# The h product of batches 6 and 7 in 512-token pieces, their loads in halves, and a new written order, in a fused linear-attention and gated-FFN kernel

## The chip, the cores and the metric

The kernel runs on one core of a Trainium2 chip. A core has five engines that run side by side, each through its own list of instructions in order: TensorE (PE, matrix products into PSUM), VectorE (DVE), ScalarE (ACT), GpSimd (POOL, which here issues the loads) and SyncE (SP, which here issues the stores). The metric is device time in microseconds for one execution. The kernel before took 179.14 us (median of 3 runs, 178.89 to 179.23).

## The reference

For 8 batches, 8 heads, 576 positions and 64 channels per head, the reference computes a linear attention, normalises it, joins the heads to 512 features, and sends the result through a feed-forward block whose gate is a convolution over three neighbouring positions:

```python
kv = np.einsum('bhsd,bhse->bhde', k, v)
out = np.einsum('bhsd,bhde->bhse', q, kv)
rms = np.sqrt(np.mean(out * out, axis=-1, keepdims=True) + 1e-06)
x = out / rms * g_norm              # heads joined: (8, 576, 512)
h = np.maximum(x @ w_in, 0.0)       # (8, 576, 1024)
conv_out = sum over k of conv_w[k] * (h moved by k - 1 positions)
gate = 1.0 / (1.0 + np.exp(-conv_out))
result = h * gate @ w_out           # (8, 576, 512), float32
```

## The kernel before, in words

**Order.** The whole program is written out by hand in one string, `ORDER` (lines 71 to 135). Each word names a function and its arguments; behind `@` stand the buffer slots that it takes, behind `!` the engine of a copy (`A` for ACT, `V` for DVE). The words are run in turn (lines 663 to 669) and each emits instructions. At the end (lines 671 to 679) the instructions of each engine are tied to that sequence, so every engine works strictly in the order of its own words. Between engines only data and buffer dependencies hold. The order comes from a search outside the kernel, which worked with a duration for every operation.

**Loads.** `Lq`, `Lk`, `Lv` (line 352) bring q, k, v of a batch from DRAM into SBUF, converted from float32 to bfloat16. With a second argument, `Lq.5.1`, one half of a batch (4 of 8 heads), otherwise the whole batch. Each of q, k and v has two slots, so a batch's load waits until the batch two or so before it in that slot has been read. `Li` and `Lo` bring the weights. All are issued by POOL, in order. The first half of batch 0 comes by another way: SP loads it as float32 into a staging tile and `ca` converts it.

**Attention.** `kv` multiplies k and v (36 small matmuls of 64x64 per half), `kvc` copies the result to SBUF, `qt` and `qc` transpose q (36 transposes per half, one copy), and `ot` (8 matmuls) gives the attention output of two head pairs in PSUM.

**Normalisation.** Batches 0 and 1 take a short way: `sq` squares (ACT), `on` sums (PE), `nl` is the reciprocal root (ACT), and `mz` scales into x (DVE). The later batches are normalised in pairs: `sq` and `oc` (ACT) square and copy the output, `ss` sums (PE), `ln` is the root (ACT), `sl` splits it into two bfloat16 parts (four DVE instructions), `sp` spreads it over the partitions (PE), and `mu` scales into x (DVE). The pairs are 2 and 3 (group 1), 4 and 5 (group 2), 6 and 7 (group 3). ACT loads one table for roots and another for the sigmoid and changes between them.

**h.** x of two batches lies in one tile of 1152 tokens. There are two ways to form h = relu(x w_in) for one block f of 128 features of the eight:

- `hm.b.f.u` (line 529): one batch, 576 tokens in two runs of 288; each `u` takes two of four contraction steps, 4 matmuls of 288 columns. It takes two PSUM banks. `re` applies the relu to 576 columns.
- `ha.p.f.e` (line 543): 512 of the pair's 1152 tokens, 4 matmuls of 512 columns, one PSUM bank; `rea` does the relu. The last 128 tokens of the pair come from `hb.p.j` (line 556), for four blocks f in one bank, 16 matmuls of 128 columns, and `reb`. The piece e=1 holds the last 64 tokens of the first batch and the first 448 of the second.

Before the change, batches 0, 1, 6 and 7 use `hm`, and the pairs p=1 (batches 2, 3) and p=2 (4, 5) use `ha` and `hb`.

**Gate.** For each group c of one or two batches (`CONV`, line 62) and each pair of feature blocks, DVE does `ta` (two scaled copies per block), `aa` and `ab` (two additions), ACT does `sg` (sigmoid), and DVE does `mg` (h times gate, in place). Groups 4 and 5 are batches 6 and 7.

**Output.** `om.p.k.i.j` (line 614) multiplies a tile of 128 tokens by half of w_out, 4 matmuls of 512 columns for i=0 (feature blocks 0 to 3) or i=1 (4 to 7). `ea` copies the finished tile into one of four row buffers in SBUF and `st` stores it, by SP. A row buffer is free again when its store has landed. The last token tile, `om.3.6`, is done in two halves of 256 columns. `sw.x.b` holds the next store back until the named load has landed. `STORES2` lists the outputs stored as two DMAs of 256 KB rather than one of 512 KB.

**Fillers.** `fi`, `fq` and `fo` are matmuls on zeros, put where PE would have nothing to do in the first part of the kernel.

Of the kernel before, what the change touches and what calls it, by code (L numbers as in the profile page):

```python
# [68 lines left out]


ORDER = """
pre@0,0,0 Lq.0.1 ca.q.0!V ca.q.1!V fi.36.128@0 fi.3.128@0 qt.0.0@0 qc.0.0!V@0 fi.1.512@2 fi.20.128@2 ct@0 ca.k.1!V
ca.k.0!A pn Lv.0.1 ca.v.0!V Lq.1.1@1 ca.v.1!A fq.1.512.0@1 fq.1.256.0@1 kv.0.0@1 Li.2 kvc.0.0!A pc fq.2.512.3@3
ot.0.0@6,4 ca.k.2!A sq.0.0@0 Li.0 fi.3.512@1 fi.2.128@1 on.0.0@0 nl.0.0@0 ca.k.3!V fq.2.512.0@2 fq.1.256.0@2 qt.0.1@2
qc.0.1!V@0 sq.0.1@0 mz.0.0@0 fi.1.512@0 fi.3.128@0 on.0.1@0 nl.0.1 fo.1.384.0.1 kv.0.1@2 kvc.0.1!V Lq.1.0 Li.3
fo.1.384.0.1 fq.1.256.1@6 ot.0.1@6,0 sq.0.2@0 mz.0.1 fq.1.512.0@2 qt.1.1@2 Li.1 Lv.1.0@1 fi.2.128@4 on.0.2@4 sq.0.3@7
nl.0.2@0 qc.1.1!V@0 fo.2.384.0.2 on.0.3@2 nl.0.3 Lk.1.0@1 fo.1.384.0.3 hm.0.5.0@4 mz.0.2 Lq.2.0@0 hm.0.4.0@2 mz.0.3
hm.0.1.0@6 hm.0.5.1 re.0.5!A@0 hm.0.4.1 ta.0.5@0 hm.0.1.1 re.0.4!A ta.0.4 qt.1.0@0 hm.0.0.0@2 hm.0.0.1 hm.0.3.0@4
hm.0.3.1 re.0.1!A ta.0.1@1 Lv.1.1 hm.0.6.0@6 qc.1.0!A@1 Lv.2.1@0 re.0.0!A aa.0.2 hm.0.2.0@0 hm.0.2.1 ab.0.2
fq.1.512.0@2 kv.1.0@2 sg.0.4 ta.0.0 re.0.3!V aa.0.0 Lk.1.1 sg.0.5 ab.0.0 kvc.1.0!A hm.0.6.1 re.0.2!A ot.1.0@4,2  # L80
hm.0.7.0@0 mg.0.2 re.0.6!V sg.0.0 Lq.3.1@1 sq.1.1@0 Lq.2.1 hm.0.7.1 ta.0.3@0 re.0.7!V ta.0.2 qt.2.0@6 qc.2.0!V@1
sq.1.0@1 aa.0.1 fo.5.384.1.1 on.1.0@0 sg.0.1 mg.0.0 nl.1.0@0 fo.5.384.1.0 on.1.1@6 nl.1.1 fo.2.384.1.0 kv.1.1@0
kvc.1.1!A fo.1.384.1.1 fq.1.256.2@6 ot.1.1@0,6 mz.1.0 mz.1.1 sq.1.2@0 qt.3.1@4 sq.1.3@1 Lk.2.1@0 qc.3.1!V@0 Lv.2.0
ab.0.1 on.1.2@2 nl.1.2@0 fo.2.384.1.2 on.1.3@4 nl.1.3 Lk.2.0 mz.1.2 fo.1.384.1.3 hm.1.7.0@2 qt.2.1@4 mz.1.3 hm.1.5.0@0
ta.0.6@1 sg.0.2 ta.0.7 hm.1.7.1 hm.1.5.1 sg.0.3 qc.2.1!V@2 re.1.7!A hm.1.1.0@6 hm.1.1.1 hm.1.4.0@4 Lv.3.1@1 re.1.1!A
hm.1.4.1 aa.0.3 mg.0.1 re.1.5!A kv.2.0@6 re.1.4!A Lo.0 hm.1.2.0@0 hm.1.2.1 ab.0.3 sg.0.6 sg.0.7 hm.1.6.0@2 ta.1.5@0
ta.1.4 Lk.3.1@1 kvc.2.0!V hm.1.6.1 Lo.1 ot.2.0@4,6 re.1.2!A re.1.6!A Lq.3.0 oc.2.1@0 kv.2.1@0 kvc.2.1!A Lq.5.0@0
hm.1.3.0@2 aa.1.2 mg.0.3 hm.1.3.1 sq.2.1@0 hm.1.0.0@0 hm.1.0.1 ta.1.7@1 sq.2.0@1 oc.2.0 ab.1.2 sg.1.5 om.0.0.0.0@7
sg.1.4 re.1.3!V ta.1.6 re.1.0!V ot.2.1@5,3 oc.2.3@1 sq.2.3@2 Lq.5.1 kv.3.1@0 om.0.0.0.1@2 aa.1.3 mg.1.2 om.0.0.1.1
Lk.3.0 sq.2.2@3 oc.2.2 kvc.3.1!V ot.3.1@0,3 ta.1.0@0 Lv.3.0 ea.0.0.1!A@0 ab.1.3 ta.1.1 qt.3.0@5 sg.1.7 sg.1.6  # L90
qc.3.0!V@0 oc.3.3@2 aa.1.0 mg.1.3 sq.3.3@4 om.0.1.1.0@2 oc.3.2 ta.1.3@1 om.0.1.0.0 ea.0.1.0!A@1 Lk.5.1@0 Lq.4.1@1
ta.1.2 om.0.1.0.1@6 om.0.0.1.0 ab.1.0 sq.3.2@5 ea.0.0.0!A aa.1.1 ab.1.1 om.0.1.1.1 sg.1.0 qt.5.1@0 qt.5.0@2 kv.3.0@4
qc.5.1!V@1 sg.1.1 ea.0.1.1!V qc.5.0!V@2 kvc.3.0!A Lq.4.0 om.0.2.1.1@7 mg.1.0 sg.1.3 sg.1.2 ot.3.0@0,4 om.0.2.1.0@6
sq.3.1@6 om.0.3.1.1@2 Lv.5.1@0 sq.3.0@7 ss.2@3 ss.3 ln.1@0 mg.1.1 oc.3.1@3 oc.3.0 sl.1@0 om.0.2.0.1 om.0.3.0.1 st.0.0
ea.0.3.1!A@2 kv.5.1@4 qt.4.1@0 Lk.5.0 sp.3.1.1@2 kvc.5.1!V Lk.4.1@1 mu.3.1.1@0 sp.2.0.1@4 mu.2.0.1 om.0.2.0.0
qc.4.1!A@0 sp.3.0.0@0 sp.3.1.0@2 ea.0.2.1!A@0 om.0.3.1.0@7 sp.3.0.1@4 mu.3.0.0 Lv.5.0 sp.2.1.1@0 mu.3.1.0 om.0.3.0.0
mu.3.0.1 sp.2.1.0@2 ea.0.2.0!A sp.2.0.0@4 mu.2.1.1 mu.2.0.0 mu.2.1.0 hb.1.0@6 Lv.4.1@1 fq.1.256.0@0 kv.4.1@0
ea.0.3.0!A kv.5.0@4 reb.1.0!A@1 kvc.5.0!V ot.5.1@6,2 kvc.4.1!A sq.5.2@0 oc.5.2@0 sq.5.3@1 ha.1.3.0@0 rea.1.3.0!V
ha.1.3.1@1 rea.1.3.1!V oc.5.3 ta.2.3@0 Lk.4.0 ot.5.0@6,4 ha.1.2.0@0 Lv.4.0 rea.1.2.0!V ha.1.2.1@3 oc.5.0@1 rea.1.2.1!V
ta.2.2 sq.5.1@2 Lk.7@0 oc.5.1 aa.2.1 ha.1.1.1@1 kv.4.0@4 sq.5.0@3 rea.1.1.1!A ot.4.1@6,2 kvc.4.0!A qt.4.0@0 oc.4.2@2  # L100
sq.4.3@4 qc.4.0!V@0 ab.2.1 oc.4.3 sq.4.2@5 ha.1.1.0@4 rea.1.1.0!A ta.2.1@1 ha.1.0.0@5 rea.1.0.0!A ha.1.0.1@2
ot.4.0@0,3 rea.1.0.1!A ta.2.0 aa.2.0 sq.4.1@6 sq.4.0@7 ha.1.6.0@5 ha.1.5.1@2 ss.4@6 oc.4.1@3 oc.4.0 ss.5 rea.1.5.1!A
ln.2@0 Lq.7@0 qt.7.1@3 qc.7.1!A@0 qt.7.0@0 om.0.4.0@2 sl.2@0 om.0.4.1 ab.2.0 ha.1.5.0@3 Lv.7@0 rea.1.6.0!A sp.5.0.1@4
sp.5.1.1@6 mu.5.0.1@1 qc.7.0!A@1 Lv.6@1 ea.0.4!A@3 sp.4.1.1@0 mu.4.1.1 ha.1.4.0@2 rea.1.5.0!A sg.2.0 hb.1.1@3 Lq.6@1
# [34 lines left out]
def kernel(  # L139
# [501 lines left out]
    def st(p, k, c=None):  # L641
# [68 lines left out]
```

## Time and profile before

| what | value |
|---|---|
| time, median of 3 runs | 179.14 us |
| the profiled execution, its own time | 179.12 us |
| its span, first to last instruction | 177.3 us |
| PE busy | 170.3 us (96%) |
| DVE busy | 157.0 us (89%) |
| ACT busy | 139.7 us (79%) |
| POOL busy (issuing loads) | 34.7 us (20%) |
| granted TensorE clock | 0.999 |

The profile gives busy times per engine, the same in 40 slices of the span, groups of instructions by source line and shape, the waits between engines, and a timeline. The duration of an instruction is longer than the distance to the next one on the same engine where the two overlap, so for an engine that works without a pause the distance from one start to the next is what an instruction costs. The 1.8 us between the span and the time lie outside the instructions.

### The profile page before, as it was taken

Reading aid. Unit: us, or ns where it says so; the run is one execution under the profiler, and the core shown is the slowest. Engines: PE = TensorE matmul, PEld = TensorE weight load, DVE = VectorE, ACT = ScalarE, POOL = GpSimd, SP = SyncE. Lnnn points to the kernel's source line nnn. Section 1 sums busy time; section 2 is a strip of 40 time slices with the busy share of each in tenths; the row PEclk is TensorE's granted clock in tenths of the full one; section 3 lists DMA queues with packets and bytes.
Section 4 is the critical chain, followed back from the end, with each engine's and each line's share of the span. In section 5 each row is a group of like instructions: output and inputs, shape, how many; then the busy total and the mean of one; then the engine's idle time right before and its main releaser. Section 6 shows DMA issues by size and latency. Waiting matters only on the chain.

```text
span 177.3 us, 5289 instructions
## 1 busy us (share of the span) xinstructions
PE 170.3 (96%) x2253; PEld 95.4 (54%) x2253; DVE 157.0 (89%) x282; ACT 139.7 (79%) x219; POOL 34.7 (20%) x60
## 2 busy tenths in 40 slices
PE   7999998899999999999999999999999999999992
PEld 7755765576444454444554454444577754444451
DVE  2757699999999796999999999999999999999931
ACT  2366799899999938999999999987795966494720
POOL 6945640851067005500000000000000000000000
PEclk9999999999999999999999999999999999999999
DMA  5999999999999996999881000005710000043594
GB/s 184 366 201 200 202 206 210 202 206 208 206 207 233 230 206 88 207 210 205 183 301 64 0 2 4 0 3 213 272 49 0 0 0 4 0 172 123 218 379 173
DMA packets 21355, 27.22 MB, mean 153 GB/s; under 512 B 1224, under 2 KB 15828, under 8 KB 21332
## 3 DMA queue, kind: packets, MB, share of 16 engines
q0 software_dynamic: 15072, 15.09, 51.5%
q1 hardware_dynamic: 6256, 11.80, 18.0%
q8 instruction: 17, 0.28, 0.6%
q14 instruction: 6, 0.05, 0.1%
q10 hardware_dynamic: 4, 0.00, 0.0%
HBM read 32.52 MB, written 9.44 MB: 237 GB/s over the span
## 4 chain that ended last, share of the span: by engine, by line
PE 66%; DVE 14%; DMA 8%; ACT 7%; issue 2%; POOL 1%; ACTq 0%; DVEq 0%
PE banks L628 28%; PE banks L534 13%; PE banks L547 12%; DMA v_sb<-in_v_dram 6%; PE banks L296 3%; PE banks L441 2%; ACT sq L448 2%; PE banks L393 2%; ACT h L238 2%; DVE xT L518 2%; DMA out_dram<-row 2%; PE banks L418 2%; DVE taps L583 2%; DVE taps L596 2%; DVE taps L584 1%
## 5 line engine op out<-in xcount | busy, mean ns | idle before, releaser
L628 PE MATMUL banks<-w_out_sb,h 128*128 128x512 bf16 x280 | 63.7, 379 | 0.2
L603 ACT ACTIVATE taps<-taps,cw 128x576 bf16<-128x576 bf16 (+1 forms) x48 | 43.6, 946 | 9.9 <-DVE taps L596 9.8
L628 PEld LDWEIGHTS <-h 128*128 128x128 bf16 x280 | 26.5, 98 | 31.5 <-issue 1.6
L238 ACT ACTIVATE h<-banks 128x512 bf16<-128x512 f32 (+1 forms) x51 | 29.8, 658 | 5.7 <-PE banks L534 4.2
L534 PE MATMUL banks<-xT,w_in_sb 128*128 128x288 bf16 x256 | 33.5, 286 | 0.4
L547 PE MATMUL banks<-xT,w_in_sb 128*128 128x512 bf16 x128 | 30.1, 379 | 0.2 <-ACT row L232 0.2
L534 PEld LDWEIGHTS <-w_in_sb 128*128 128x128 bf16 x256 | 24.6, 98 | 8.3 <-issue 1.6
L232 ACT ACTIVATE row<-banks 128x512 f32<-128x512 f32 (+1 forms) x29 | 16.8, 601 | 9.6 <-PE banks L628 5.6
L590 DVE TENSOR_TENSOR taps<-taps 128x1152 bf16<-128x1152 bf16 (+1 forms) x24 | 22.9, 956 | 0.5
L596 DVE TENSOR_TENSOR taps<-taps,h 128x1152 bf16<-128x1152 bf16 (+1 forms) x24 | 22.8, 952 | 0.3
L609 DVE TENSOR_TENSOR h<-h,taps 128x1152 bf16<-128x1152 bf16 (+1 forms) x24 | 22.7, 951 | 0.2 <-ACT taps L603 0.2
L583 DVE TENSOR_SCALAR taps<-h,cw 128x576 bf16<-128x576 bf16 (+1 forms) x48 | 20.3, 423 | 1.7 <-ACT h L238 1.5
L448 ACT ACTIVATE sq<-banks 128x576 bf16<-128x576 f32 x32 | 20.4, 674 | 1.7 <-PE banks L441 1.7
L584 DVE TENSOR_SCALAR taps<-h,cw 128x576 bf16<-128x576 bf16 (+1 forms) x48 | 20.1, 418 | 0.0
L547 PEld LDWEIGHTS <-w_in_sb 128*128 128x128 bf16 x128 | 11.8, 98 | 14.4 <-issue 1.3
L518 DVE SCALAR_TENSOR_TENSOR xT<-o,cw,banks 128x576 bf16<-128x576 f32 x24 | 18.1, 806 | 0.4 <-PE banks L511 0.3
L232 ACT ACTIVATE o<-banks 128x576 f32<-128x576 f32 x24 | 15.9, 678 | 0.0
L240 DVE TENSOR_SCALAR h<-banks 128x576 bf16<-128x576 f32 (+1 forms) x17 | 12.2, 720 | 1.1 <-PE banks L547 1.0
L354 POOL DMA_DIRECT2D k_sb<-in_k_dram x12 | 8.7, 726 | 20.0 <-PE banks L441 9.4
L227 ACT ACT_TABLE_LOAD x8 | 10.3, 1283 | 2.1 <-issue 2.0
L354 POOL DMA_DIRECT2D v_sb<-in_v_dram x13 | 9.4, 724 | 11.2 <-PE banks L324 4.7
L354 POOL DMA_DIRECT2D q_sb<-in_q_dram x13 | 9.6, 738 | 7.5 <-PE banks L418 6.5
(74 smaller groups left out, 149.1 us busy)
## 6 DMA issues: line engine op xcount, KB each, us to landing
out_dram<-row SPq DMA_DIRECT2D x10, 512.0 KB, 2.8
out_dram<-row SPq DMA_DIRECT2D x15, 256.0 KB, 4.1
q_sb<-in_q_dram POOLq DMA_DIRECT2D x11, 288.0 KB, 10.6
v_sb<-in_v_dram POOLq DMA_DIRECT2D x11, 288.0 KB, 10.7
k_sb<-in_k_dram POOLq DMA_DIRECT2D x10, 288.0 KB, 10.8
stg<-in_k_dram SPq DMA_DIRECT2D x2, 576.0 KB, 6.0
k_sb<-in_k_dram POOLq DMA_DIRECT2D x2, 576.0 KB, 10.1
q_sb<-in_q_dram POOLq DMA_DIRECT2D x2, 576.0 KB, 9.9
```

The lines of the kernel that those rows point to most:

```text
L232: nc.scalar.activation(to, fr, AX.Copy)
L238: nc.scalar.activation(to, fr, AX.Relu)
L354: loads[x, b] = nc.gpsimd.dma_start(out=qkv(x, b)[:, w0:w0 + n, :], in_=rows(x, b, w0, n))
L448: nc.scalar.activation(by_r(s), natural(T["ot", b, t][:, :S]), AX.Square)
L534: nc.tensor.matmul(ps[:, e, :HS], w_in_sb[:, t, f * P:(f + 1) * P], x[:, t, e * HS:(e + 1) * HS], start=(t == 0), stop=(t == NT - 1))
L547: nc.tensor.matmul(ps, w_in_sb[:, t, f * P:(f + 1) * P], x[:, t, e * 512:(e + 1) * 512], start=(t == 0), stop=(t == NT - 1))
L583: nc.vector.tensor_scalar_mul(tap[:, 0, f % 2, :n, 8:8 + S], h[:, f], cw[:, f:f + 1])
L590: nc.vector.tensor_add(tap[:, 1, :, :n, :S], tap[:, 0, :, :n, 7:7 + S], tap[:, 1, :, :n, 1:1 + S])
L596: nc.vector.tensor_add(y, y, h[:, 2 * j:2 * j + 2])
L603: nc.scalar.activation(y, y, AX.Sigmoid, scale=scale)
L609: nc.vector.tensor_mul(h, h, T["tap", c, j][:, 1, :, :n, :S])
L628: nc.tensor.matmul(ps[:, 0], h[:, f, m * P:(m + 1) * P], w_out_sb[:, f, :], start=first and f == 4 * i, stop=not first and f == 4 * i + 3)
```

## The change

The code of the functions is the same; two lists that the kernel reads, `STORES2` and `ORDER`, are changed (`HALF` and `PAIRH` are read by nothing in the kernel).

- The h of batches 6 and 7 is formed as the pair p=3 by `ha`/`rea` (16 pieces of 512 tokens) and `hb`/`reb` (2 pieces of 128 tokens for four blocks each), in place of 32 `hm` and 16 `re`.
- q, k and v of batches 6 and 7 are loaded in halves, 12 loads in place of 6, and `kv` and `kvc` of these batches are done in halves too.
- The order of all words is new, with other slots, other engines for some copies and fillers of other sizes. The first `st.0.0` and `st.0.2` are held until the load of v of batch 4 has landed; `st.0.4` is held until k of batch 6 has; the other holds are gone.

The core of the diff, with the parts of `ORDER` at the start, at the normalisation of batches 6 and 7, and at the end:

```diff
-HALF = [0, 1, 2, 3, 4, 5]
+HALF = [0, 1, 2, 3, 4, 5, 6, 7]
-PAIRH = [1, 2]
+PAIRH = [1, 2, 3]
-STORES2 = [(0, 0), (0, 3), (0, 2), (0, 1)]
+STORES2 = [(0, 0), (0, 2), (0, 1), (1, 0)]
...
-ot.0.0@6,4 ca.k.2!A sq.0.0@0 Li.0 fi.3.512@1 fi.2.128@1 on.0.0@0 nl.0.0@0 ca.k.3!V fq.2.512.0@2 fq.1.256.0@2 qt.0.1@2
-nl.0.2@0 qc.1.1!V@0 fo.2.384.0.2 on.0.3@2 nl.0.3 Lk.1.0@1 fo.1.384.0.3 hm.0.5.0@4 mz.0.2 Lq.2.0@0 hm.0.4.0@2 mz.0.3
-ab.0.1 on.1.2@2 nl.1.2@0 fo.2.384.1.2 on.1.3@4 nl.1.3 Lk.2.0 mz.1.2 fo.1.384.1.3 hm.1.7.0@2 qt.2.1@4 mz.1.3 hm.1.5.0@0
-ta.0.6@1 sg.0.2 ta.0.7 hm.1.7.1 hm.1.5.1 sg.0.3 qc.2.1!V@2 re.1.7!A hm.1.1.0@6 hm.1.1.1 hm.1.4.0@4 Lv.3.1@1 re.1.1!A
...
-mu.3.0.1 sp.2.1.0@2 ea.0.2.0!A sp.2.0.0@4 mu.2.1.1 mu.2.0.0 mu.2.1.0 hb.1.0@6 Lv.4.1@1 fq.1.256.0@0 kv.4.1@0
...
-sq.6.2@6 sq.6.3@7 om.1.0.1.1 om.1.4.1@1 om.1.0.1.0@5 sg.3.7 ea.1.0.1!A@2 ss.6@6 ss.7 ta.3.0 aa.3.0 ab.3.0 om.1.3.1.1@4
-om.1.0.0.0 mg.3.3 ta.3.3@1 om.1.3.0.1 ln.3@0 sl.3@0 ea.1.0.0!A om.1.3.1.0@7 ea.1.3.1!V@3 ea.1.2.0!A oc.6.2 sp.6.0.1@5
...
-om.3.1.1.0 om.3.0.1.1 ea.3.1.0!V sg.5.1 ea.3.0.1!V sg.5.3 mg.5.1 st.3.1 om.3.3.1@2 om.3.4.1@0 sg.5.0 st.3.0 om.3.2.1@1
-mg.5.0 ea.2.0.1!V st.2.0 om.3.4.0 ea.3.4!A@1 om.3.2.0 om.3.5.0 ea.3.2!V@3 om.3.3.0 st.3.4 st.3.2 ea.3.5!A@2 st.3.5
-ea.3.3!V@0 st.3.3 om.3.6.1@0 ea.3.6.1!V@1 st.3.6.1 om.3.6.0 ea.3.6.0!A@3 st.3.6.0
+fq.1.256.1@1 ot.0.0@6,4 sq.0.0@0 fi.3.512@1 fi.2.128@1 on.0.0@0 sq.0.1@7 nl.0.0@0 fi.1.512@2 on.0.1@2 nl.0.1 mz.0.1@0
+nl.0.3 fo.1.384.0.3 hm.0.4.0@6 hm.0.5.0@4 mz.0.2 Lq.1.0 qt.1.0@0 mz.0.3 hm.0.5.1 Li.0 qc.1.0!V@1 Li.1 hm.0.4.1
+ot.1.1@0,4 qc.3.1!V@0 Lv.2.1@0 sq.1.3@0 qt.2.1@2 qc.2.1!V@2 sq.1.2@1 on.1.3@6 nl.1.3@0 aa.0.1 Lk.2.0@0 mz.1.3
+fo.1.384.1.2 on.1.2@2 nl.1.2 fo.1.384.1.2 hm.1.5.0@6 Lk.2.1 mz.1.2 hm.1.1.0@2 hm.1.3.0@4 hm.1.3.1 ab.0.1 Lv.2.0 ta.0.6
...
+ea.0.2.0!A sp.2.1.0@3 mu.2.1.0 sp.2.0.0@6 hb.1.0@5 sw.v.4 st.0.0 ea.0.3.0!A reb.1.0!A@1 mu.2.0.0 fq.1.512.0@0 kv.4.1@0
+kv.5.0@2 ot.5.1@4,6 kvc.4.1!A oc.5.2@0 ha.1.2.0@0 ha.1.2.1@1 sq.5.3@0 oc.5.3 kvc.5.0!V ot.5.0@2,6 sw.v.4 st.0.2
...
+mg.2.2 ha.2.4.1@1 rea.2.5.1!A rea.2.4.1!A rea.2.0.0!A om.1.3.0.1@7 ot.6.0@5,3 sq.6.1@4 oc.6.1@2 sq.6.0@5 kv.6.1@1
+om.1.0.0.0@0 ta.3.1@1 om.1.3.1.1 ta.3.0 kvc.6.1!A ot.6.1@1,3 oc.6.0 aa.3.0 om.1.0.1.0 sq.6.3@6 om.1.1.0.0@5 ta.3.6
+ab.3.0 sq.6.2@7 ss.6@6 ss.7 ln.3@0 sl.3@0 ea.1.3.1!V@1 sw.k.6 st.0.4 om.1.1.1.0 ea.1.0.0!A@0 ea.1.1.0!A@3 oc.6.3@3
+oc.6.2 om.1.1.1.1@6 om.1.1.0.1 sp.6.1.1@4 ea.1.1.1!A sp.7.1.0@0 sp.7.1.1@2 mu.7.1.1@0 sg.3.1 om.1.0.0.1@7 om.1.2.0.0@6
...
+om.3.2.1@6 ea.2.2.1!A ea.3.0.0!A@3 om.3.1.0.0 sg.5.2 st.2.1 mg.5.0 sg.5.3 st.2.2 mg.5.1 om.3.5.0 om.3.4.0 ea.3.0.1!V
+st.3.0 om.3.3.1@7 om.3.3.0 ea.3.4!V@0 om.3.1.1.1 ea.3.5!A@2 ea.3.3!V@1 ea.3.1.1!V@3 ea.3.1.0!A om.3.2.0 st.3.4 st.3.5
+ea.3.2!V@0 st.3.3 st.3.1 st.3.2 om.3.6.1@0 ea.3.6.1!V@2 om.3.6.0 st.3.6.1 ea.3.6.0!A@1 st.3.6.0
```

The loads of POOL from batch 4 on, in their new order: `Lk.4.0 Lq.7.0 Lk.5.0 Lk.4.1 Lv.4.1 Lq.4.0 Lv.4.0 Lv.7.1 Lq.7.1 Lk.7.1 Lv.7.0 Lk.7.0 Lq.6.0 Lk.6.0 Lv.6.0 Lv.6.1 Lq.6.1 Lk.6.1`; before, `Lk.4.1 Lv.5.0 Lv.4.1 Lk.4.0 Lv.4.0 Lk.7 Lq.7 Lv.7 Lv.6 Lq.6 Lk.6`.

## The prediction

> **What bounds the kernel now.** I read the busy times and the slices first, then busy time by stretch, then groups by shape, the chain that ended last, and the timeline where the chain changes engine.
>
> ```profile
> PE 170.3 (96%) x2253; PEld 95.4 (54%) x2253; DVE 157.0 (89%) x282; ACT 139.7 (79%) x219; POOL 34.7 (20%) x60
> PE   7999998899999999999999999999999999999992
> DVE  2757699999999796999999999999999999999931
> ```
> PE is full from start to end and DVE nearly so. By stretch (start:end, length, then busy us of PE, PEld, DVE, ACT, POOL):
>
> ```profile
> 16.50:35.30 18.80, 17.72 (x332) 11.50 (x332) 17.17 (x32) 16.20 (x24) 8.90 (x14) 1.00 1.25 205
> ...
> 66.20:106.00 39.80, 39.49 (x693) 20.53 (x693) 37.69 (x55) 38.84 (x65) 4.47 (x6) 1.00 0.69 142
> ...
> 126.70:173.90 47.20, 47.16 (x281) 27.16 (x278) 42.96 (x78) 29.73 (x46) 0.00 (x0) 1.00 0.27 101
> ```
> In the first of these PE is full partly of fillers; behind 35.3 it is full of work. From 66 to 106 ACT is full too. The chain, in order of time (start, length, what):
>
> ```profile
> 34.48 0.81 DVE xT L470
> ...
> 55.74 10.40 DMA v_sb<-in_v_dram
> ...
> 126.71 15.97 PE banks L534 x128
> 142.68 26.85 PE banks L628 x124
> 169.53 0.03 ACTq L232
> ```
> The last line of `mz` (L470) ends at 35.29 and `hm.1.7.1` starts at 35.30: up to here DVE sets the pace. Behind it the chain is mostly PE. The load that lands at 66.14 (55.74 + 10.40) releases `kv.4.1` at 66.19. L534 x128 is the h of batches 6 and 7, 15.97 us. The tail, from the timeline:
>
> ```profile
> 171.95 1.91 PE L621 MATMUL banks<-w_out_sb,h 128*128 128x256 bf16 x16
> 173.67 0.42 DVE L234 COPY row<-banks 128x256 f32<-128x256 f32 x1 [0.51 <-DMA out_dram<-row]
> 174.28 0.38 ACT L232 ACTIVATE row<-banks 128x256 f32<-128x256 f32 x1 [2.40 <-DVE row L234]
> ```
> PE ends at 173.86, and the last copies wait for row buffers whose stores still land.
>
> **Costs.** PE is in order and full, so I price its work by the distance from one word's start to the next, in the trace (medians): `hm` 490 ns, `ha` and `om` 862 to 864, `hb` 986, half a `kv` 355 with no gap, a whole one 710. For DVE and ACT likewise: relu of 512 columns 477 on ACT and 600 on DVE, of 576 columns 530 (547 median) and 668; `kvc` 160 and 205.
>
> **The h of batches 6 and 7.** PE: 32 `hm` x 0.490 = 15.68 us go; 16 `ha` x 0.864 + 2 `hb` x 0.986 = 13.82 + 1.97 = 15.80 come. That is +0.12 us on the full engine: the columns are the same, and pieces of 128 columns are dear. Relu: 12 x 0.530 + 4 x 0.668 go (12 on ACT and 4 on DVE), 16 x 0.477 + 2 x 0.600 come: 9.0 us become 8.8, 1.3 more on ACT and 1.5 less on DVE, beside PE in a stretch (126 to 143) where ACT is not full. So this part alone brings nothing. It lets the evictions take single banks, but every e=1 piece needs `mu` of both batches.
>
> **The whole sum per engine**, both orders priced with the same costs: PE 160.65 before and 160.79 after (fillers 10.23 and 10.28 of these); DVE 152.83 and 151.01 (four `kvc` and four `re` fewer, two `rea` and one `ea` more); ACT 133.36 and 135.01 (`kvc` 14 for 8, more relus). Both orders change the ACT table seven times. Since PE is bound, the change is worth what it saves in PE's lost time: in the profiled execution PE's last matmul ends at 173.86, 13.2 us behind its own sum (its lag), of which 9.0 stand at 35.30 and 4.2 come later in pieces of 0.05 to 0.3 us.
>
> **Start to the first h of batch 1.** The first data are unchanged (staging lands at 4.60, 6.09, 8.03; `Lv.0.1`, still second, at 13.08). `ca.q.0` and `qc.0.0` move from DVE to ACT, which idled 2.9 and 1.3 us there for the stagings. `sq.0.1` now stands ahead of `nl.0.0`, so `nl.0.1` can start about 1 us earlier, but `mz.0.2` and `mz.0.3` still hang on `Lv.0.1`. Hence `re.0.5` and the first `ta` stay near 19.5. `qc.1.0` moves into DVE's 1.46 us wait ahead of it: hidden, provided `Lq.1.0` lands as fifth load by 17.7 (the fourth landed at 15.67, and loads took 1.4 to 1.9 us each there: 17.1 to 17.6). `Li.0` becomes sixth (19.00) and is wanted at 19.1. From the first `ta` to the last `mz` DVE has 14.95 us of work before (15.76 real) and 14.85 after, so with the same 0.8 lost the last `mz` ends at 35.2; with none lost, at 34.3. Following ACT and PE to it word by word (`nl.1.2` done at 33.75) gives 34.7. I take 34.95, between: `hm.1.3.1` at 34.97 against 35.30, with 134.36 us of PE behind it against 134.33. **-0.33 us, bounds -1.0 and +0.1.**
>
> **35 to 66 us: loads and stores.** Loads land one after the other, a half of a batch per 1.41 us. `st.0.0` went out at 52.8 and the two loads around it landed 2.6 and 2.5 us after their predecessors. The new order holds `st.0.0` until v of batch 4 has landed, so `Lv.4.1` (37th rather than 36th) should land at about 65 and not 66.14, with `kv.4.1` due at about 65.7. The filler and wait ahead of it, 0.39 us, become one filler of 0.22: **-0.17 us**, bounds -0.4 and 0.
>
> **Loads of 6 and 7 in halves.** Twelve issues for six: 6 x 0.72 = 4.3 us more of POOL, which waits 9.4 us in this region and issues nothing later. First landing: `Lq.7.1`, second in the queue behind a release at 67.3, by about 73.5 alone (first landing of that stage before: 5.95 us after issue, then 2.8 per whole, 1.4 per half); the three stores now released at 67.7 (1.5 MB, some 4 us of the DMA engines at the 380 GB/s of the late slices) can push it to 77.5. `qt.7.1` wants it at 67.2 + 12.0 = 79.2 (PE's sum plus its lag there). Cost 0. Four `kv` halves for two wholes: 4 x 0.355 against 2 x 0.710, or 4 x 0.409 with the median: **+0.1 us**, bounds 0 and 0.2.
>
> **Normalisation of 6 and 7.** PE's distance from the end of `ot.6.1` to the first `sp.6` shrinks from 7.4 to 4.8 us of words. The path between is `sq` 0.53 + `sq` 0.66 + table 1.28 + `ln` 0.50 + `sl` 1.76 + some 0.2 of handing over = 4.9. PE waits 0.1 there, as before (0.16 at 119.3). **0 us**, if ACT is on time. DVE waits some 2.8 us for `ln.3` (1.2 before), covered at the end: it finishes `mg.5.1` at about 165.5 and PE wants it at 153.9 + 13.1 = 167.0; before, it was 0.2 us ahead of PE.
>
> **Tail.** `ea.3.6.0` still waits for a row whose store (`st.3.3`) goes out about 2.5 us ahead of PE's end; stores of 256 KB took 1.7 to 3.3 us to land, so it starts between 0.05 and 0.5 us behind PE's end (0.42 before); `st.3.1`, 512 KB, is now among the last. **0 us, bounds -0.35 and +0.35.**
>
> **Sum**, against the profiled execution's 179.12 (the median of the runs is 179.14): 179.12 - 0.33 - 0.17 + 0.10 + 0.03 = 178.75, **178.7 us**.
>
> **A rule against the trace.** Halves land 1.41 us apart and wholes 2.81 (73.29, 76.11, 78.92): halving costs the queue nothing. The Trainium skill, page DMA: Bandwidth & Descriptors, section Anatomy of one DMA, gives each such DMA a fixed part of about 2.0 us beside its bytes; were that paid in line, the eleven loads from `Lv.7.1` on would take an estimated 3.4 us each and `Lq.6.1`, the tenth, would land at about 101.7, four microseconds behind its need, for a sum of some 182.9 us.
>
> **Rivals.** About 0.36 us (0.2%) is what a measurement can tell from no change.
> - *Gains swallowed*: DVE loses its 0.8 us again and `Li.0` or the first PE words are late by tenths; 179.1 to 179.3. For it: PE's sum is 0.14 larger and the fillers are as long.
> - *ACT late at batch 6 (slower).* ACT has 39.2 us of words from `reb.1.0` (at 65.4) to `sq.6.1` (36.9 before, done in 38.9). With the same 2.0 us lost it arrives at 106.6, 0.9 ahead of the end of `ot.6.0` (107.5). If it loses over 2.9 us, each further one is paid by PE at `sp.6.1.1`, and queued behind that are the rest of `om.1` and all of `ha.3`. Losing 4.4 gives 178.7 + 1.5 = 180.2. For it: ACT waited 9.8 us for `taps` in all. Against it: in 66 to 106 it was busy 38.84 of 39.80 us.
> - *Stores against loads of 7*: if `Lq.7.1` lands 1 us behind 79.2, PE waits at `qt.7.1`: 179.7.
> - *Fixed cost per load in line*: 5.95 - 2.8 = 3.1 us per load by the rows above would bring the tenth load at 67.3 + 10 x 4.5 = 112, 15 us late: 194 us; the 1.41 us between halves speaks against it.
> - *Larger gain*: no DVE loss up to `mz` (34.3) and half of PE's some 1.8 us of plain waits behind 35 gone, 179.12 - 1.0 - 0.5 = 177.6.
>
> **How the numbers follow.** Forecast 178.7 (own range 178.4 to 179.1) 0.45, of which 0.36 is below 178.76; larger gain 0.11; swallowed 0.17, of which 0.13 is within; ACT late 0.20; stores 0.06; fixed cost 0.01. Faster 0.47, same 0.22 (0.09 + 0.13), slower 0.31. The range leaves out half of the larger gain and half of the slow cases: 177.7 to 180.2.
>
> **What would show it.** `hm.1.3.1` starting at 34.6 to 35.2; no wait of PE at `kv.4.1`; L547 x192 and no L534 behind 100 us; `sp.6` within 0.2 us of the words before it; PE's last matmul at 173.3 to 173.7 and `ea.3.6.0` within 0.5 of it. A PE gap at `sp.6`, at `qt.7.1` or between 16 and 35 us would make me wrong.

## The result and the profile after

The changed kernel took 181.2 us (median of 6 runs, 180.75 to 182.06) where the kernel before took 179.14 beside it: a ratio of 1.0122, 95% interval 1.0093 to 1.0151. A repeat gave 181.15 and 1.0094 (1.0066 to 1.0123). So the change costs 1.7 to 2.2 us; I had forecast a gain of 0.4. The profiled execution took 181.26 us with a span of 179.5, against 179.12 and 177.3. Four runs of the kernels below, of 183.1 to 186.6 us at a granted clock of 0.978 to 0.990, were in a slower state and are left out of the times and ratios.

The page of the changed kernel: busy time per engine, then the shares of the chain that ended last, then two groups (line, engine, operation, count | busy us, mean ns | idle us before them).

```profile
PE 171.5 (96%) x2178; PEld 87.2 (49%) x2178; DVE 155.6 (87%) x277; ACT 142.6 (79%) x228; POOL 39.1 (22%) x66
PE 39%; DVE 37%; ACT 10%; DMA 5%; issue 4%; POOL 2%; POOLq 0%; ACTq 0%; DVEq 0%
L547 PE MATMUL banks<-xT,w_in_sb 128*128 128x512 bf16 x192 | 44.5, 379 | 0.0
L534 PE MATMUL banks<-xT,w_in_sb 128*128 128x288 bf16 x128 | 17.3, 286 | 0.2 <-ACT o L463 0.2
```

The pieces are there (192 matmuls of L547 for 128 before), PE is as full as before, and behind 20 us no wait of it is longer than 0.41 us. What changed is the chain: on the page of the kernel before, PE held 66% of it and DVE 14%, here 39% and 37%. By stretch, with the columns of the prediction:

```profile
16.50:35.30 18.80, 17.73 (x331) 11.26 (x332) 17.43 (x33) 15.64 (x25) 9.77 (x14) 1.00 1.25 205
66.20:106.00 39.80, 39.53 (x662) 20.30 (x660) 37.15 (x52) 38.46 (x65) 7.89 (x11) 1.00 0.68 134
126.70:173.90 47.20, 47.07 (x244) 22.21 (x242) 43.28 (x79) 32.49 (x51) 0.00 (x0) 1.00 0.31 115
```

Busy shares hardly differ, so they do not show the loss. It shows in PE's lag: the start of a word minus the sum of the prices of all PE words ahead of it, taken at the same amount of PE work done.

| PE work done, us | lag before | lag after | difference |
|---|---|---|---|
| 12 | 5.87 | 6.52 | +0.65 |
| 34 | 9.72 | 9.92 | +0.20 |
| 46 | 10.52 | 11.48 | +0.96 |
| 56 | 11.32 | 12.11 | +0.79 |
| 100 | 12.60 | 13.80 | +1.20 |
| 140 | 12.99 | 14.11 | +1.12 |
| 156 | 13.02 | 14.35 | +1.33 |
| end | 13.21 | 14.54 | +1.33 |

PE's last matmul ends at 175.33 instead of 173.86: 0.14 from its larger sum and 1.33 from lag. The last store lands at 178.58 instead of 176.41, 3.25 us behind PE instead of 2.55: another 0.70. The rows of the main places follow.

**Start.** The chain of the changed kernel (start, length, what):

```profile
5.92 8.91 DMA q_sb<-in_q_dram
14.87 0.68 PE banks L418 x36
15.65 0.77 DVE qT L234
16.93 0.75 ACT o L463
19.41 0.66 ACT h L238
20.09 0.37 DVE taps L583
...
35.09 0.81 DVE xT L470
35.90 0.67 DVE taps L596
```

`qt.1.1` (L418) starts as `Lq.1.1` lands, at 14.83. Its copy `qc.1.1` frees the bank that `on.0.3` needs, `nl.0.3` (L463) ends at 17.67 (17.11 before), and the first `ta` starts at 20.09 (19.52). From there DVE is busy for 15.63 of 15.81 us, and the last `mz` (L470) ends at 35.90 (35.28).

**The output of batch 0.** PE's one long wait, and what DVE did ahead of it (timeline):

```profile
56.16 1.89 PE L628 MATMUL banks<-w_out_sb,h 128*128 128x512 bf16 x8 [0.41 <-DVE qT L234]
54.68 0.76 DVE L596 TENSOR_TENSOR taps<-taps,h 128x1152 bf16<-128x1152 bf16 x1
55.36 0.75 DVE L234 COPY qT<-banks 128x1152 bf16<-128x1152 bf16 x1
```

`om.0.2.1.1` waits for a bank that the copy `qc.5.0` (L234) empties, and that copy stands behind `ab.1.1` (L596).

**End.** DVE's last gate `mg.5.1` is late because it waits for its sigmoid on ACT, and PE waits 0.22 us for it at `om.3.4.0`. Then the last matmuls, the copies on ACT, and the DMA engines (last two columns: their busy share, GB/s):

```profile
167.84 0.76 DVE L609 TENSOR_TENSOR h<-h,taps 128x1152 bf16<-128x1152 bf16 x1 [0.84 <-ACT taps L603]
172.74 0.60 ACT L232 ACTIVATE row<-banks 128x512 f32<-128x512 f32 x1 [2.79 <-DMA out_dram<-row]
173.42 1.91 PE L621 MATMUL banks<-w_out_sb,h 128*128 128x256 bf16 x16
175.37 0.39 ACT L232 ACTIVATE row<-banks 128x256 f32<-128x256 f32 x1 [2.03 <-PE banks L621]
170.00:174.00 4.00, 4.00 (x23) 2.06 (x22) 2.45 (x4) 0.60 (x1) 0.00 (x0) 1.00 0.99 373
```

The last copy (175.37) starts 0.04 us behind PE and waits for no row. Its store goes out at 175.78 and lands 2.80 us later; before, the last store took 1.72. The DMA engines are full from 170 to 174 us.

### The profile page after: what moved, and what is told of

Same layout as the page of the kernel before. It is cut to its first block, busy times and chain, and to the rows that moved or that the text cites. A ratio compares the mean times of both kernels' runs of the same rounds, so it can differ in the third digit from the quotient of the medians.

```text
span 179.5 us, 5145 instructions
## 1 busy us (share of the span) xinstructions
PE 171.5 (96%) x2178; PEld 87.2 (49%) x2178; DVE 155.6 (87%) x277; ACT 142.6 (79%) x228; POOL 39.1 (22%) x66
## 4 chain that ended last, share of the span: by engine, by line
PE 39%; DVE 37%; ACT 10%; DMA 5%; issue 4%; POOL 2%; POOLq 0%; ACTq 0%; DVEq 0%
PE banks L628 19%; PE banks L547 9%; DVE taps L590 6%; DVE h L609 5%; DVE taps L596 5%; DMA q_sb<-in_q_dram 5%; DVE taps L584 5%; DVE taps L583 5%; DVE h L240 3%; DVE xT L518 3%; DVE qT L234 3%; PE banks L562 3%; ACT h L238 2%; ACT row L232 2%; PE banks L393 2%
## 5 line engine op out<-in xcount | busy, mean ns | idle before, releaser
L628 PE MATMUL banks<-w_out_sb,h 128*128 128x512 bf16 x280 | 64.6, 379 | 0.8 <-DVE qT L234 0.4
L547 PE MATMUL banks<-xT,w_in_sb 128*128 128x512 bf16 x192 | 44.5, 379 | 0.0
L238 ACT ACTIVATE h<-banks 128x512 bf16<-128x512 f32 (+1 forms) x55 | 31.0, 625 | 5.4 <-PE banks L547 2.4
L547 PEld LDWEIGHTS <-w_in_sb 128*128 128x128 bf16 x192 | 18.0, 98 | 21.4 <-issue 1.3
L232 ACT ACTIVATE row<-banks 128x512 f32<-128x512 f32 (+1 forms) x28 | 15.7, 595 | 10.1 <-PE banks L628 5.2
L596 DVE TENSOR_TENSOR taps<-taps,h 128x1152 bf16<-128x1152 bf16 (+1 forms) x24 | 22.9, 954 | 0.3
L534 PE MATMUL banks<-xT,w_in_sb 128*128 128x288 bf16 x128 | 17.3, 286 | 0.2 <-ACT o L463 0.2
L354 POOL DMA_DIRECT2D q_sb<-in_q_dram x15 | 11.0, 735 | 16.2 <-PE banks L418 10.8
L534 PEld LDWEIGHTS <-w_in_sb 128*128 128x128 bf16 x128 | 12.1, 98 | 4.7 <-issue 1.5
L354 POOL DMA_DIRECT2D v_sb<-in_v_dram x15 | 10.9, 728 | 11.3 <-PE banks L393 8.9
L354 POOL DMA_DIRECT2D k_sb<-in_k_dram x14 | 10.1, 720 | 12.0 <-PE banks L393 7.2
L240 DVE TENSOR_SCALAR h<-banks 128x512 bf16<-128x512 f32 (+1 forms) x15 | 10.5, 706 | 1.0 <-PE banks L547 1.0
```

Source lines behind the costliest of these rows:

```text
L232: nc.scalar.activation(to, fr, AX.Copy)
L238: nc.scalar.activation(to, fr, AX.Relu)
L354: loads[x, b] = nc.gpsimd.dma_start(out=qkv(x, b)[:, w0:w0 + n, :], in_=rows(x, b, w0, n))
L534: nc.tensor.matmul(ps[:, e, :HS], w_in_sb[:, t, f * P:(f + 1) * P], x[:, t, e * HS:(e + 1) * HS], start=(t == 0), stop=(t == NT - 1))
L547: nc.tensor.matmul(ps, w_in_sb[:, t, f * P:(f + 1) * P], x[:, t, e * 512:(e + 1) * 512], start=(t == 0), stop=(t == NT - 1))
L596: nc.vector.tensor_add(y, y, h[:, 2 * j:2 * j + 2])
```

## The experiments

Ratios are to the kernel before, run beside each kernel; times of the changed kernel for comparison are 181.15 to 181.2.

### The whole again, and halves of the order

The two kernels once more, and two orders put together at the first `hm.1` (what one order has not done by then follows in the other's order):

```diff
# start_before
-words of the order after, up to the first hm.1
+words of the order before, up to the first hm.1
# start_after
-words of the order before, up to the first hm.1
+words of the order after, up to the first hm.1
```

> The changed kernel as it is. In its first trace the load Lq.1.1 landed at 14.83 us (14.33 in the kernel before, although the four loads up to it are issued in the same order at the same times), qt.1.1 stands on it, and the chain runs on from there. Theory A (a wait that is in the order): Lq.1.1 lands at 14.7 to 14.9 again, the first ta starts at 20.0 to 20.1, PE's last matmul ends near 175.3. Theory B (a landing that differs from one execution to the next): Lq.1.1 lands anywhere from 14.3 to 14.9, the first ta moves with it, and the whole time by the same amount. In both, the last store lands about 3.2 us behind PE's last matmul (2.55 before).

> The kernel before as it is, for a second trace of its landings. Theory A: Lq.1.1 at 14.3 and the first ta at 19.5 again. Theory B: Lq.1.1 between 14.3 and 14.9, the first ta with it, and the time 0 to 0.6 us longer than 179.1.

> The order of before up to its first hm of batch 1, then all that the new order has left. If the loss of 2.1 us lies in the start (0.6 us of lag at that point), the time is 180.5; if it lies in the middle (0.75 us of lag that comes between 35 and 170 us) and the tail (0.7 us), 0.6 less than the changed kernel at most. If the new rest only fits its own start, 181 or more.

> The new order up to its first hm of batch 1, then all that the order of before has left (batches 6 and 7 by hm, their loads whole). If the start loses 0.6 us and the rest keeps before's pace, 179.7 to 179.8; if the start costs nothing, 179.1; if the middle of before only fits its own start, 180.2 or more.

Measured: after_again 181.15 us (above); before_again 179.25, 0.9996 (0.9982 to 1.001); start_before 183.65 (two runs), 1.0233 (1.0158 to 1.0308); start_after 181.82, 1.0118 (1.0083 to 1.0153). In after_again `Lq.1.1`, issued alike, landed at 14.45, the first `ta` started at 19.75 and the last `mz` ended at 35.59: part of the late start differs from execution to execution. Over all profiles here that share one of the two starts, the first `ta` began at 19.44 to 20.81 in the order before (nine profiles, median 19.76) and at 19.75 to 20.35 in the order after (eight, 20.06), and the last `mz` ended at 35.11 to 36.30 (seven, 35.39) and at 35.59 to 36.45 (six, 35.92). So the new order starts later by some 0.3 to 0.5 us, and the 0.6 of the two profiles above is partly chance. From the first `ta` to the last `mz` the ranges do not meet: 15.49 to 15.77 us before and 15.81 to 16.10 after. The hybrids are no better than the wholes that they are made of, so this cut tells no part apart: an order's second half is written for its own first half.

### The parts of the change in the order before

The pieces alone: each pair of `hm.6`/`hm.7` words gives its place to one `ha.3`, its relu keeps its engine. Then the same with all relus on ACT, and the halves alone.

```diff
# pieces_alone (example)
-hm.6.4.0@0 ... hm.6.4.1 ... re.6.4!A
+ha.3.6.0@0 ... rea.3.6.0!A
# pieces_act, besides
-rea.3.2.0!V rea.3.3.1!V rea.3.0.0!V rea.3.5.1!V
+rea.3.2.0!A rea.3.3.1!A rea.3.0.0!A rea.3.5.1!A
# halves_alone (six of these)
-Lq.7@0
+Lq.7.1@0 Lq.7.0
```

> The kernel before, its order and its whole loads kept; only the h product of batches 6 and 7 is done in 512-token pieces: each pair of hm.6/hm.7 words gives its place to one ha.3 piece, in its first bank, and two hb.3 words of 128 tokens follow. Theory A (the pieces by themselves cost what my sum says, +0.12 us of PE, and the loss of the changed kernel comes from its new order): 179.1 to 179.4 us, the last matmul within 0.3 us of 173.9. Rival B (the pieces themselves cost, because they join batch 6 to batch 7 and the taps of chunk 4 wait for pieces that hold both): 180.5 us or more, the last matmul at 175 or later, with idle time of PE between 130 and 150 us.

> The kernel before with the 512-token pieces for batches 6 and 7 as tried alone, now with all of their relus on ACT; there four were on DVE and PE stood 1.0 us for them between 134 and 139 us. Theory A (the pieces cost nothing but the order must carry their relus, which a piece needs twice as long as one batch's 288 before its bank comes free): 179.2 to 179.5 us and no wait of L547 over 0.2 us. Rival B (the pieces cost by themselves, since a piece's bank is held longer whoever empties it): 179.8 us or more, with the wait now on ACT.

> The kernel before, its order kept; only the six loads of batches 6 and 7 are each issued as two halves, one directly behind the other, where the whole was. Theory A (halves cost nothing that PE sees): 178.9 to 179.4 us. Rival B (a fixed cost of each load on POOL or its queue pushes the loads back or takes DMA time from the stores): 179.7 us or more, with kv.7 or qt.7.1 waiting for a DMA.

Measured: pieces_alone 180.06 us, 1.0041 (1.0027 to 1.0055), between the two theories; pieces_act 179.43, 1.0008 (0.9997 to 1.0019); halves_alone 179.34, 1.0004 (0.9992 to 1.0017), which is +0.07 us (-0.14 to +0.30). In pieces_alone, by groups from 125 to 152 us and by the chain there:

```profile
L547 PE MATMUL banks<-xT,w_in_sb 128*128 128x512 bf16 x67 | 15.4, 379 | 1.1 <-DVE h L240 1.0
134.44 1.26 DVE taps L596
135.71 0.60 DVE h L240
136.31 1.26 DVE h L609
137.57 0.28 DVE taps L583
137.85 0.28 DVE taps L584
138.13 0.61 DVE h L240
138.79 2.75 PE banks L547 x12
```

A relu of a piece (L240) on DVE stands behind `ab` and `mg` of 1.26 us each, and PE waits for its bank. With these relus on ACT the wait is gone (timeline of pieces_act):

```profile
131.26 8.87 PE L547 MATMUL banks<-xT,w_in_sb 128*128 128x512 bf16 x38
```

So neither the pieces nor the halves cost anything of note, if ACT takes the relus. The halves also settle the rule that the prediction weighed: the Trainium skill, page DMA: Bandwidth & Descriptors, section Anatomy of one DMA, gives a DMA on this path a fixed part of about 2.0 us. The same section says that this is mostly the wait for completion, and the trace agrees that transfers in a queue do not pay it one after the other: in halves_alone two neighbouring halves landed at 77.30 and 78.71, 1.41 us apart, and the last load at 88.95 where the last whole one of the kernel before landed at 88.69.

Then the held store of the fourth step alone, and everything together in the order before:

```diff
# before_hold
-om.0.3.0.1 st.0.0 ... Lv.4.1@1
+om.0.3.0.1 ... Lv.4.1@1 sw.v.4 st.0.0
-ea.0.2.1!A@0 ... ea.0.4!A@3
+ea.0.2.1!A@3 ... ea.0.4!A@0
# parts_in_before: before_hold + pieces_act + halves_alone
```

> The kernel before with one store moved: st.0.0 waits for the first half of v of batch 4, as in the kernel after, and rows 0 and 3 change places for two tiles. Theory A of my forecast's fourth step (the store in the way makes that load late): the load lands at 65.0 to 65.6 instead of 66.1 and the time falls by 0.1 to 0.3 us, to 179.0 to 179.2. Rival B (the load's landing comes from its place in the queue, not from the store): landing unchanged within 0.2 us, time 179.2 to 179.4. A rise over 0.2 us would mean that the store is missed later.

> The kernel before, its written order kept, with all the parts of the change that can be done without a new order: the 512-token pieces for batches 6 and 7 (their relus on ACT), the loads of batches 6 and 7 in halves, and st.0.0 held behind the first half of v of batch 4. Theory A (the parts cost nothing and the hold gains as it did alone; the whole loss of the changed kernel is its order): 178.8 to 179.2 us. Rival B (the parts cost only together, because the halves land in other work than the pieces leave room for): 179.8 us or more.

Measured: before_hold 178.89 us, 0.998 (0.9968 to 0.9992); parts_in_before 178.77, 0.9972 (0.9957 to 0.9987). In before_hold `Lv.4.1` landed at 64.07 instead of 66.14, and `kv.4.1` (L393) follows its filler (L317) at once:

```profile
65.94 0.30 PE L317 MATMUL banks<-zero 64*64 64x256 bf16 x2
65.96 0.93 PE L393 MATMUL banks<-v_sb,k_sb 64*64 64x64 bf16 x72
```

The gain was expected at 0.1 to 0.3 us and came as 0.1 to 0.6. parts_in_before, faster than both kernels, is where my forecast for the whole change stood, but by luck: its parts were priced at +0.12, 0 and -0.17 us, and it has nothing of the start that made up the rest. It does not contain the `kv` of 6 and 7 in halves, which I did not try alone. So what costs 2 us is the new order, with its slots and engines, and at most a small part of it those `kv`.

### The bank wait at om.0.2.1.1

The kernel after, `qc.5.0` ahead of `ab.1.1` on DVE:

```diff
-kvc.3.0!A ab.1.1 sg.1.1 ot.3.0@0,5 qc.5.0!V@1
+kvc.3.0!A qc.5.0!V@1 ab.1.1 sg.1.1 ot.3.0@0,5
```

> The kernel after, with one DVE copy moved: qc.5.0 now stands ahead of ab.1.1 on DVE rather than behind it, so that the bank that om.0.2.1.1 needs comes free some 0.7 us earlier. Theory A (PE's wait of 0.4 us at om.0.2.1.1 is lost for good, since PE has no later wait that would swallow it): 0.3 to 0.5 us below the kernel after, 180.7 us or a little less, and no wait for qT at L628 near 56 us. Rival B (DVE, not PE, sets the pace again behind 150 us, so the gain ends in om.3.5.0 and om.3.4.0 waiting longer for mg.5.1): within 0.15 us of the kernel after, with the wait at om.3.4.0 grown by 0.4 us.

Measured: 182.5 us, 1.0174 (1.0144 to 1.0204), 1.3 us worse. Both theories fell. The timeline of wait_fix:

```profile
55.61 0.75 DVE L596 TENSOR_TENSOR taps<-taps,h 128x1152 bf16<-128x1152 bf16 x1
56.39 1.44 ACT L603 ACTIVATE taps<-taps,cw 128x576 bf16<-128x576 bf16 x2 [0.87 <-DVE taps L596]
58.42 0.43 PE L484 MATMUL banks<-sq,sel 128*32 128x288 bf16 x8 [0.43 <-ACT sq L448]
62.12 0.30 PE L511 MATMUL banks<-wparts,spread 32*128 32x288 bf16 x4 [0.39 <-DVE wparts L502]
```

The wait at `om.0.2.1.1` is gone (PE's lag there fell by 0.42), but `ab.1.1` ends 0.9 us later. Behind it hang ACT's two sigmoids, its last square, the table change, the root and DVE's four parts, and PE now waits for the square (L484) and for the parts (L511). In the kernel after that path ended at 61.06 and PE wanted it at 61.2. PE, DVE and ACT were level here; the copy behind `ab.1.1` was the cheaper of two waits.

### Slack behind the start

One DVE instruction less in each kernel (the output lacks that tap); then a delay in each, of four fillers (0.64 us) in the order before and five (0.80 us) in the order after.

```diff
# after_less, before_less
-ab.0.0
# before_delay
-fo.1.384.0.3
+fo.5.384.0.3
# after_delay
-fo.1.384.0.3
+fo.6.384.0.3
```

> The kernel after without one DVE instruction, ab.0.0 (the centre tap of features 0 and 1 of batch 0, some 0.7 us near 22 us; the output lacks that tap), all else kept. Theory A (in the kernel after DVE's row of work sets the pace from the first tap at 20 us to the norm's parts at 61 us, with nothing behind it to take up a gain or a delay): the spread of the norm starts 0.5 to 0.7 us earlier and the time falls by 0.4 to 0.7 us against the kernel after, to about 180.5. Rival B (PE sets it, DVE has room): within 0.2 us of the kernel after.

> The kernel before without the same DVE instruction, ab.0.0. Theory A (in the kernel before PE waits for the load of v of batch 4 at 66.1 us, whose landing the queue sets, so what comes earlier or later by some 0.4 us ahead of it is swallowed there): 179.1 to 179.4 us, no gain over 0.2 us, and the wait ahead of kv.4.1 grown from 0.2 to 0.7 us or so. Rival B (both kernels pass a gain or a delay on alike): 178.6 to 178.8 us, as much below as the kernel after without it.

> The kernel before with four more filler matmuls of 384 columns (0.16 us each, results unused) ahead of the first hm word: the first tap is 0.6 us later, at some 20.15 us. Theory A (this order has slack behind its start: it waits for v of batch 4 near 66 us anyway): 179.4 to 179.7 us, so at most two thirds of the delay reach the end. Rival B (the delay reaches the end whole): 179.9 us or more.

> The kernel after with five more such filler matmuls at the same place; PE comes to hm.0.5.0 some 0.6 us later. Theory A (this order has no slack behind its start, PE, DVE and ACT run level from 20 to 61 us and the load of v of batch 4 has long landed): the delay reaches the end whole, 0.5 to 0.7 us above the kernel after, 181.7 to 181.9 us. Rival B (it has as much slack as the kernel before): 181.2 to 181.5 us.

Measured: after_less 180.35 us, 1.0066 (1.0054 to 1.0078), 0.8 below the kernel after; before_less 179.25, 1.0004 (0.999 to 1.0019); before_delay 179.55, 1.0004 (0.999 to 1.0018); after_delay 181.77, 1.0149 (1.0122 to 1.0176), 0.6 above the kernel after.

By the medians the delays came out as the theory of slack had them: of 0.64 us, 0.1 to 0.25 reach the end in the order before, and of 0.80 about 0.6 in the order after. The intervals are wide (-0.2 to +0.3 us by the ratio in the order before), and the traces do not show the mechanism. With the load long landed (before_hold), PE went from the filler ahead of `kv.4.1` to `ot.5.1` in 0.75 us; in before_again, before_less and before_delay it took 0.83 to 0.84, in the kernel before 1.02. So the wait for `Lv.4.1` cost 0.1 to 0.3 us, too little to swallow 0.6. Nor does anything behind it swallow a delay: from the first `sp` (L511) to PE's last matmul the order before took 113.38 to 113.45 us in six profiles, before_delay among them, though its `sp` began 0.50 later than in the kernel before; the order after took 114.06 to 114.13 in six, after_delay among them. PE's last matmul ended 0.45 us later in before_delay and 0.49 later in after_delay than in the profile of each kernel without the delay. That the order before has the more slack is therefore not shown. In before_less, too, the gain was gone at its first `sp` (60.48, 60.40 in the kernel before), ahead of the load.

after_less gave the number of theory A, but not by its way. Its last `mz` ended 15.7 us behind its first `ta`, as in the kernel after (15.8). The chain in after_less:

```profile
21.95 0.77 DVE taps L596
22.74 0.78 ACT taps L603
23.52 0.54 ACT h L238
24.27 0.44 PE banks L441 x8
24.71 1.09 PE banks L534 x8
...
28.39 0.77 ACT L227
29.68 0.75 ACT o L463
31.19 0.81 DVE xT L470
```

With 0.7 us of DVE gone, ACT's sigmoid and relu, PE's `ot` and `hm`, and ACT's table and root carry the chain to the same `mz`: DVE was not the bound alone. PE's last matmul ended at 175.02 (175.33 in the kernel after, 174.91 in after_again). Most of the gain stood at the end, where the last store landed 2.39 us behind PE instead of 3.25, its flight being 1.94 us. The section on the end shows why.

### The end

Three kernels, all the kernel after: its last copies and stores in another order, one 512 KB store left out far ahead of the end, and one left out close to it.

```diff
# tail_new (core)
-om.3.1.0.0 ... st.2.2 mg.5.1 ... ea.3.0.1!V st.3.0 ... om.3.1.1.1 ... st.3.4 st.3.5 st.3.3 st.3.1 st.3.2
+om.3.1.0.0 om.3.1.1.1 ... st.2.2 st.3.0 mg.5.1 ea.3.1.1!V@2 ea.3.1.0!A st.3.1 ... st.3.5 ... st.3.4 ... st.3.3 st.3.2
# after_short
-st.2.2
# after_short31
-st.3.1
```

> The kernel after, with the order of its last evictions and stores changed and nothing else: om.3.1.1.1 and ea.3.0.1 earlier, st.3.0 and the 512 KB st.3.1 earlier, each of st.3.5, st.3.4, st.3.3, st.3.2 directly behind its own eviction. Theory A (0.7 us of the loss is the stores that come too late and stand in one another's way, so that the last one takes 2.8 us instead of 1.7): the last matmul as in the kernel after (174.9 to 175.4), the last store landed 2.4 to 2.8 us behind it instead of 3.25, so 0.5 to 0.9 us below the kernel after. Rival B (the last store's time does not depend on the stores ahead of it): within 0.2 us of the kernel after and the last store still 3.1 us or more behind the last matmul.

> The kernel after without one store, st.2.2 (512 KB; those rows of the output are not written), all else kept. From 170 to 176 us the profile of the kernel after shows the DMA engines 87 to 99 per cent busy. Theory A (the stores not yet sent at 165 us, 3.75 MB against 3.25 MB before, fill the DMA engines, and the end waits for them): the last store lands 2.2 to 2.6 us behind the last matmul instead of 3.25 and the time falls by 0.6 to 0.9 us against the kernel after, to 180.2 to 180.5; PE ends as before. Rival B (the last two stores pay a latency that no other store changes): 181.0 us or more.

> The kernel after without one store, st.3.1 (512 KB, sent at 173.5 us with only st.3.2 and the two halves of the last tile behind it; those rows of the output are not written). Taking st.2.2 away, six stores further ahead, left the last four stores as they were. Theory A (the last store's flight of 2.8 us, 1.7 before, is made by the 512 KB sent 2.3 us ahead of it, which the order puts there): the last store flies 1.6 to 1.9 us, lands 2.2 to 2.5 us behind the last matmul, and the time falls by 0.7 to 0.9 us against the kernel after, to 180.3 to 180.6. Rival B (something other than the stores ahead makes it): 181.0 us or more.

Measured: tail_new 180.49 us, 1.0066 (1.0044 to 1.0087), 0.66 below the kernel after; after_short 181.36, 1.0115 (1.0093 to 1.0137), no gain; after_short31 180.59, 1.0065 (1.0042 to 1.0089), 0.56 below. The stretch from 170 us in after_short has the DMA engines only 77% busy:

```profile
170.00:174.00 4.00, 4.00 (x22) 1.96 (x21) 2.22 (x4) 0.78 (x2) 0.00 (x0) 1.00 0.77 290
```

Yet its last store took 2.8 us as before the edit. In after_short31 it took 2.1, more than the 1.6 to 1.9 that I expected, in tail_new 1.7 (issue to landing). So it is not the bytes left at 165 us, as I had it. The 512 KB of `st.3.1`, sent at 173.5, 2.3 us ahead of the last store, are a part of it; `st.3.1` is that late because its copy waits for row 3 (the 2.79 us at 172.74 above). But after_less sends `st.3.1` as close ahead of its last store, and that store took only 1.94 us. What differs there is a packet of another DMA queue, q14, which the profile lists as instruction. In the kernel after, one such packet of 8 KB starts at 177.02, while the last store is in flight; in after_less it comes at 178.86, behind it. The queue in both (packets, MB, share of 16 engines), kernel after from 176 to 178.5 us and after_less from 178 to 180:

```profile
q14 instruction: 1, 0.01, 0.8%
q14 instruction: 1, 0.01, 1.9%
```

And the DMA engines (last two columns) at the end of the kernel after, then of after_less:

```profile
175.80:177.40 1.60, 0.00 (x0) 0.00 (x0) 0.00 (x0) 0.00 (x0) 0.00 (x0) 1.00 0.93 322
177.40:178.10 0.70, 0.00 (x0) 0.00 (x0) 0.00 (x0) 0.00 (x0) 0.00 (x0) 0.82 0.07 13
175.50:177.10 1.60, 0.00 (x0) 0.00 (x0) 0.00 (x0) 0.00 (x0) 0.00 (x0) 1.00 0.92 321
177.10:177.80 0.70, 0.00 (x0) 0.00 (x0) 0.00 (x0) 0.00 (x0) 0.00 (x0) 0.62 0.00 0
```

Behind 177.4 the kernel after has one engine's worth of work left (a share of 0.07 is one of 16), and its last packet ends at 178.13; in after_less all are done at 177.06. The flight of the last store in all 19 profiles:

| | q14 packet outside the flight | inside |
|---|---|---|
| no 512 KB store within 4 us ahead | 1.71 to 1.80 us (nine profiles) | 2.04 to 2.12 (after_short31, pieces_act, start_after) |
| `st.3.1` 2.2 to 2.7 us ahead | 1.94 (after_less, start_before) | 2.80 to 2.85 (after, after_again, after_short, after_delay, wait_fix) |

So the long flight needs both: the store alone adds 0.2 us, the packet alone 0.3 to 0.4, the two together 1.1. Taking either away brings most of it back. In the five profiles with both, the packet came 1.69 to 1.75 us behind PE's last matmul; in the kernel before it came 2.15 ahead of it. What sets its time no run shows.

tail_new moved `st.3.1` and also met no packet in flight, so its gain does not tell the two apart. It does not gain all of it: its last copy waits for a row and starts at 176.15, 0.61 behind PE:

```profile
176.15 0.38 ACT L232 ACTIVATE row<-banks 128x256 f32<-128x256 f32 x1 [4.74 <-DMA out_dram<-row]
```

## Why the prediction was wrong, step by step

- **The h of 6 and 7, +0.12 us:** right within the noise (pieces_act +0.14, -0.05 to +0.34), and "this part alone brings nothing" holds. The price of `hb` was too high for these pieces: the two `hb.3` took 0.894 us each in the changed kernel, not 0.986. The step left out who empties the banks: with four relus on DVE it costs 0.73.
- **Whole sum per engine:** the sums stand, but "the change is worth what it saves in PE's lost time" was then filled with two places only. PE's lag grew from 13.2 to 14.5 in small pieces that I had not looked for.
- **Start, -0.33 us:** this step failed, with the wrong sign. `hm.1.3.1` began at 35.98, not 34.97. "The first `ta` stay near 19.5" rested on `Lv.0.1`, the wrong load: it landed at 12.42, sooner than before, and the chain came by another. In the new order `hm.0.5.0` needs `nl.0.3`, not `nl.0.2`, and `nl.0.3` hangs on `Lq.1.1` through `qt.1.1`, `qc.1.1` and a bank. (In tail_new, where `Lq.1.1` landed at 14.04, the chain came instead by the staged half of v, landed at 8.36, and the first `ta` was no sooner, 20.35.) Of the 0.8 us that DVE had lost to `mz`, none came back (15.81 us from the first `ta` to the last `mz`, 15.76 before).
- **35 to 66 us, -0.17 us:** the mechanism was right: `Lv.4.1` landed at 65.00 as said, and PE did not wait for it; alone, the hold gains 0.1 to 0.6. But PE came to `kv.4.1` at 66.62, later than the 66.19 of the kernel before, because of what it had lost by then (in after_again, with its sooner start, at 66.20).
- **A wait that I had not seen:** `om.0.2.1.1`, 0.41 us, which no step priced. I had followed data and loads, not the banks.
- **Loads in halves, 0, and `kv`, +0.1:** the loads were right (halves_alone +0.07, -0.14 to +0.30; `Lq.7.1` at 77.75, PE needed it later); `kv` alone was not measured.
- **Normalisation, 0:** right, 0.14 us at `sp.6.1.1`, so the rival of ACT late at batch 6 did not come. Its second half failed: `mg.5.1` began at 167.84 and PE waited 0.22, where I had it done at 165.5, as I had counted DVE's work and not its wait for ACT's sigmoid.
- **Tail, 0 (bounds -0.35 and +0.35):** failed, +0.70. The row wait that I priced was gone; the flight of the last store, which had no term in the sum, grew from 1.72 to 2.80 us. I had noted `st.3.1` among the last and given it no price, and had not looked at queue q14. It repeats: 3.25 and 3.30 us from PE to the last landing in the two profiles of the changed kernel, 2.55 and 2.55 before.

The 1.33 us of lag, by the table: 0.20 is left at 34 us of work; 0.76 comes from 34 to 46, of which 0.41 is the wait at `om.0.2.1.1`; 0.17 goes again up to 56, where the kernel before waits for its load; 0.41 comes up to 100 and 0.21 from 140 to 156, the latter at `mg.5.1`, and 0.08 goes between. What comes between 56 and 100 us of work no experiment took apart. In after_again PE's last matmul ended 0.42 us sooner than in the changed kernel's profile, at 174.91, and it was as much ahead at `kv.4.1` already: that part of the 1.33 belongs to one execution.

## What to carry to other kernels

Try the parts of a change in the old order before you judge a new one: here each part that was tried was free or a gain there, and the new order cost 2 us. Where several engines are level, a wait taken away can come back elsewhere, as at `om.0.2.1.1`; look in the chain for how many engines it passes through. Before you say that a wait takes up delays, measure it: here it cost 0.1 to 0.3 us. At the end of a kernel, look at the size of the stores that go out in the last 3 us and at what other queues send while the last store is in flight, not at the number of stores. And take a second profile of the same kernel before you explain 0.4 us.

## What was not expected of the hardware

`Lq.1.1`, issued at 5.8 to 5.95 us in all profiles, landed between 14.04 and 14.87. The store `st.0.0`, held back, let `Lv.4.1` land 2.1 us sooner, though the DMA engines were shown as full with and without it. The last store, 128 KB, took 1.71 to 2.85 us to land, by whether 512 KB had been sent in the 2.7 us ahead of it and whether one 8 KB packet of queue q14 came while it was in flight; the packet left one of the 16 DMA engines working 0.7 us longer than the others.
